# Weight and activation loads of a fused attention and feed-forward kernel put into one gated sequence, with longer and fewer filler matmuls at the start

## The chip, the cores and the metric

The kernel runs on one core of one Trainium2 chip. The metric is device time in microseconds (us) of one execution. A profile is one execution recorded by the hardware profiler; its times count from the first instruction of the span. TensorE is PE (its weight loads are PEld), VectorE is DVE, ScalarE is ACT, GpSimd is POOL, SyncE is SP. SP and POOL issue the DMAs: SP's go through the hardware queue (q1 in the profile), POOL's through the software queue (q0). KB are counted as written to the chip's memory.

## What is computed

Linear attention with a decay per head, in blocks of 64 positions, for 4 batches, 8 heads, 768 positions and a head size of 64, then a feed-forward layer over the 3072 tokens:

```python
for b in range(nb):                                   # blocks of 64 positions
    intra = einsum('bhic,bhjc->bhij', qb, kb) * Dmask
    intra = einsum('bhij,bhjd->bhid', intra, vb)
    inter = einsum('bhid,bhde->bhie', qb * lam_pow, kv_state)
    out[:, :, sl] = intra + inter
    kv_state = lam_block * kv_state + einsum('bhsd,bhse->bhde', kb * rev_pow, vb)
x = out.transpose(0, 2, 1, 3).reshape(3072, 512)
h = x @ w_in                                          # 512 x 2048
g = where(h >= 1, h, where(h <= -1, 0, (h + 1) ** 2 / 4))
y = g @ w_out                                         # 2048 x 512
```

## The kernel before

**Tiling.** Tokens go in 24 chunks `c` of 128; two neighbouring chunks are a pair `m` (0 to 11), which is the unit of loading; four chunks are a stage `s` (0 to 5), the unit of the feed-forward layer. For each pair there are three loads, q, k and v, 512 KB each (`f_load`, L552 for q and L557 for k and v), each into a ring of three buffers. The weights come in eight slices of 512 KB as bf16, converted on the way from float32 by POOL's DMAs: four of w_in (`load_w_in`, L163) by output columns, here called w_in 0 to 3, and four of w_out (`load_w_out`, L167) by rows, w_out 0 to 3.

**Attention of a pair.** q is scaled and cast (`cast_q`, L300), k likewise (`cast`, L292), on DVE or POOL; v is cast on ACT (`cast_v`, L315). In the first three pairs q and k are transposed on PE (`f_tq` L329, `f_t` L322) and copied out by ACT and DVE (`f_qT` L332, `f_kT` L336); later pairs are transposed by DMAs that SP issues (`f_qx` L343, `f_kx` L340). PE then makes the state update `u` (L401; DVE adds it to the state, L407 and L409, ACT copies the state out, L416), the scores in two parts, called A (the first chunk, with half of the state's contribution, L360 and L372) and B (the second chunk); DVE masks the scores (L421); C multiplies by v (L388); ACT copies the result to xT (`f_x`, L428). For a pair in `MERGED` the update u is issued in the same piece as the C of the pair before.

**Feed-forward of a stage.** The first layer (`f_l1`, L439) uses one w_in column tile at a time and writes PSUM tile ph, of which there are two; ACT makes r out of it (L448), DVE makes g in three steps t, w and gT (L458, L464, L469), with three buffers each; the second layer (`f_l2`, L487) accumulates a chunk's 16 row tiles in PSUM tile py, four for each w_out slice; ACT copies it out (L492) and SP stores it. In stage 0 the first layer is done for half a stage (one pair, 256 columns) and one w_in slice at a time, in the order of `L0` (L72). Such a group is 16 matmuls. Below, "group (p, w)" is half p with slice w.

**Order of the work.** Nothing is scheduled by hand in the text: every piece of work is an `Op` (L176) with an engine, a duration, needs and a due time, and `run_plan` (L198) plays them through, always taking the ready one with the earliest due time, and then issues them in that order. Engines run their instructions in that order. `D0` gives the due times of the first four chunks, `l_due` those of the feed-forward pieces, `LEAD`, `APART`, `QXD`, `KXD`, `AD`, `BD` how far ahead of them the attention pieces are due, `LDD` how far ahead the loads. A wrong duration in this plan costs no correctness, only an order that does not suit the chip.

**Loads.** `ORDER` (L69) is the sequence of the first loads: a number is a pair's three loads, a tuple `(0, i)` or `(1, i)` a slice of w_in or w_out. `GATE` (L73) makes one DMA wait until another has landed (`f_load` and `f_w` add that dependency): w_in 0 waits for the q load of pair 1, pair 2's q load for w_in 0, w_out 0 for w_in 2, w_out 2 and pair 3's loads for w_out 0. `W_AFTER` (L196) puts a slice behind a POOL cast.

**Filler matmuls.** In the first 18 us of the plan, `run_plan` fills the idle time of PE in the plan with matmuls of the identity (`warm`, L269 to L274, 256 columns): 80% of the gap at 107 ns each. There are 68 of them, 23 before the first transposes.

Of the kernel before, what the change touches and what calls it, by code (L numbers as in the profile page):

```python
# [23 lines left out]
def kernel(  # L24
# [16 lines left out]
    nc = tc.nc  # L41
# [21 lines left out]
    XT = 6  # L63
    NQT, NQK, RING = 4, 4, 3
    W_IN = (4, 4, 4, 4)
    MERGED = tuple(range(5,12))
    SWITCH = 96
    W_OF = [i for i, n in enumerate(W_IN) for _ in range(n)]
    ORDER = [0, 1, (0, 0), (0, 1), (0, 2), (0, 3), 2, (1, 0), (1, 1), 3, (1, 2), (1, 3)]  # L69
    D0 = (8350, 10000, 15450, 17000)  # L70
    FIRST = [(0, 2), (2, 4)]
    L0 = [(0, 0), (0, 1), (0, 2), (0, 3), (1, 0), (1, 1), (1, 2), (1, 3)]  # L72
    GATE = {(0, 0): ('lq', 1), 2: 0, (1, 0): 2, 3: 4, (1, 2): 4}  # L73
    LORD = {}
    DBG = False

    const = ctx.enter_context(tc.tile_pool(name="const", bufs=1))
# [107 lines left out]

    MMS, FETCH = {"s": 16, "u": 8}, 1300
    FIRST_BYTE = 2750
    LDD, STD = 16000, 3000
    QXD, KXD = 7000, 7000
    AD, BD = (8000, 4000), (4000, 2000)  # L190
    UD, TD = (9000, 9000), (8000, 8000)
    KT_ACT = (1,)
    K_DVE = (0,1,2,3,5)
    ON_DVE = ((0,0),(0,1),(2,1))
    SHARED = (1,(0,1))
    W_AFTER = {1: ("cq", 1, 0)}  # L196

    def run_plan(free):  # L198

        users = {x.key: [] for x in ops}  # L200
        for x in ops:
            x.needs = [OPS[y] for y in x.keys if y in OPS]
            for y in x.needs:
                users[y.key].append(x)
        left = {x.key: len(x.needs) for x in ops}
        topo = [x for x in ops if not x.needs]
        for x in topo:
            for u in users[x.key]:
                left[u.key] -= 1
                if left[u.key] == 0:  # L210
                    topo.append(u)
        assert len(topo) == len(ops)
        for x in reversed(topo):
            d = [u.due - u.ns - x.extra - LAT for u in users[x.key] if not u.dma]
            x.due = min(d + ([x.own] if x.own is not None else []), default=1e9)
            if x.dma or x.key[0] in ("l1", "l2"):
                x.due = x.own
        left = {x.key: len(x.needs) for x in ops}
        ready = {e: [] for e in free}
        for x in topo:  # L220
            if not x.needs:
                ready[x.eng].append((0, x))
        out_seq, xfer, dma_free, fetched = [], [0] * RING, FIRST_BYTE, 0
        while len(out_seq) < len(ops):
            t, e = min((max(free[e], min(r for r, _ in lst), xfer[-RING] if e == "SP" else 0), e)
                       for e, lst in ready.items() if lst)
            r, x = min(((r, x) for r, x in ready[e] if r <= t), key=lambda p: (p[1].due, p[0]))
            ready[e].remove((r, x))
            ns = x.ns + (720 if x.perf and free["POOL"] > t else 0)
            free[e] = t + ns  # L230
            x.t, x.end = t, t + ns + x.extra
            if e == "PE":
                n = fetched + 2 * MMS.get(x.key, MMS.get(x.key[0], 4))
                if n // 256 > fetched // 256:
                    dma_free = max(dma_free, t) + FETCH
                fetched = n
            if x.dma:
                dma_free = max(dma_free, t + (1300 if e == "SP" else 2100)) + x.dma
                x.end = dma_free + (400 if x.key[0] in ("lk", "lv", "lq") and x.key[1] < CPS // 2 else 1000 if x.key[:2] == ("w", 0) else 1400)
                if x.key[0] in ("lk", "lv", "lq") and x.key[1] >= FAR // 2:  # L240
                    x.end += SLACK if x.key[1] >= 5 else NEAR
                if e == "SP":
                    xfer.append(dma_free)
            out_seq.append((t, len(out_seq), x))
            for u in users[x.key]:
                left[u.key] -= 1
                if left[u.key] == 0:
                    ready[u.eng].append((max(y.t if y.eng == u.eng and y.key != u.gate else y.end + (XSL if u.eng == "SP" and y.eng == "POOL" and u.dma in (640, 1280) else LAT) for y in u.needs), u))
        pe_end = WARM[0]
        for t, _, x in sorted(out_seq, key=lambda p: p[:2]):  # L250
            if x.eng == "PE" and pe_end is not None:
                n = int((t - pe_end - 50) * WARM[3] / WARM[2])
                if t > WARM[1]:
                    pe_end = None
                else:
                    pe_end = t + x.ns
                    if DBG and n > 0:
                        print(f"{t / 1e3:9.3f} 0 WARM {n} {x.key}")
                    warm(max(n, 0))
                    if x.key in (("s", 1), ("C", 0)):  # L260
                        hot[0] = None
            if DBG:
                print(f"{t / 1e3:9.3f} {x.due / 1e3:9.3f} {x.eng:5s} {x.ns:6.0f} {x.key}")
            x.fn()

    WARM = (2700, 18000, 107, 0.8)
    hot = [None]

    def warm(n):  # L269

        for _ in range(n):
            if hot[0] is None:
                hot[0] = pp_h.tile([128, MS], F32, name="ph", tag="ph")
            nc.tensor.matmul(hot[0][:, :256], lhsT=ident, rhs=_bc(ident, 1, 2), start=True, stop=True)  # L274

    def mm(*cols):
        return sum(c / 2.4 + 3 for c in cols)
# [232 lines left out]


    T0, STEP = 22000, 1075
    LEAD, APART = 6000, 3000
    PARTS = {1: 2, 2: 2, 4: 1}
    EARLY = 3
    parts = {s: [slice(p * MS // n, (p + 1) * MS // n) for p in range(n)] for s in range(NST) for n in (PARTS.get(s, 1),)}
    parts[0] = [slice(a * C, b * C) for a, b in FIRST]

# [28 lines left out]
    def f_load(c, x, wait):  # L547
        b, s0 = c // NCB, (c % NCB) * C
        if x == 0:
            t = lq.tile([128, H, 2, D], F32, name="x0f", tag="x0f")  # L550
            i = q[b, :, s0:s0 + 2 * C, :].rearrange("h (j e) d -> j h (e d)", e=2)
            d = nc.sync.dma_start(out=t.rearrange("p h e d -> p h (e d)"), in_=i)  # L552
            qkv_ld[c // 2, 0] = t
        else:
            t = ld.tile([128, H, 2, D], F32, name=f"x{x}f", tag=f"x{x}f")
            i = (k, v)[x - 1][b, :, s0:s0 + 2 * C, :].rearrange("h (j e) d -> j h (e d)", e=2)
            d = nc.sync.dma_start(out=t.rearrange("p h e d -> p h (e d)"), in_=i)  # L557
            for e in range(2):
                qkv_ld[c + e, x] = t[:, :, e]
        ld_dma["lq lk lv".split()[x], c // 2] = d.ins.name  # L560
        if wait is not None:
            tc.add_manual_dep(d.ins, w_dma[wait].ins.name, SYNC)

    def f_w(it, wait):
        (load_w_in, load_w_out)[it[0]](it[1])
        if wait is not None:
            tc.add_manual_dep(w_dma[-1].ins, ld_dma[wait] if isinstance(wait, tuple) else w_dma[wait].ins.name, SYNC)


    order = list(ORDER)  # L570
    order += [m for m in range(NCH // 2) if m not in order]

    w_seen, last_c, pos_ = [], None, 0
    for it in order:
        if isinstance(it, tuple):
            gated = GATE.get(it)
            need = [("w",) + w_seen[-1] if w_seen else None, W_AFTER.get(len(w_seen))]
            key = None
            if gated is not None:
                key = gated if isinstance(gated, tuple) else ("w",) + w_seen[gated]  # L580
                need.append(key)
            add(("w",) + it, "POOL", 900, lambda it=it, wait=gated: f_w(it, wait), need, due=pos_ * 1e-3,
                dma=2560)
            if key is not None:
                OPS[("w",) + it].gate = key
            w_seen.append(it)
            pos_ += 1
            continue
        m, gated = it, GATE.get(it)
        od = o_due(2 * m + 1)  # L590
        for x in LORD.get(m, (0, 1, 2)):
            need = [("w",) + w_seen[gated] if gated is not None else ("w",) + w_seen[-2] if len(w_seen) > 1 else None]
            need += [[("cq", m - LQ, 0), ("cq", m - LQ, 1), ("cq", m - LQ, 9)], [("cast", 2 * (m - LD) + 1, 1), ("cast", 2 * (m - LD) + 1, 9)],
                     [("cast", 2 * (m - LD) + 1, 2)]][x]
            add(("lq lk lv".split()[x], m), "SP", 700, lambda m=m, x=x, wait=gated: f_load(2 * m, x, wait), need,
                due=pos_ * 1e-3 if m < EARLY else od - LDD, dma=1850)
            pos_ += 1

    NPB = NCH // 2
    for m in range(NPB):  # L600
# [155 lines left out]
```

## Time and profile before

| | |
|---|---|
| median of 13 runs | 220.34 us (218.81 to 221.85) |
| the profiled execution's own time | 219.83 us |
| its span | 218.1 us, so 1.7 us lie around it |
| PE busy | 206.9 us (95%) |
| DVE, ACT, POOL busy | 150.3, 115.2, 59.9 us |
| first matmul of the first layer | 19.57 us |
| DMA, share of 16 engines by q1 and q0 | 62.3% and 11.8% |
| x0f (q) loads, waited for by POOL's casts | 33.5 us in 8 waits |
| granted TensorE clock | 1.0 |

A busy PE is not PE at its peak, and fillers count as busy. DMA issue times stand on the issuing engine; the time from issue to landing of a single DMA is read by asking for its tile in a window that holds only that issue.

### The profile page before, as it was taken

How to read it: one execution, taken by the hardware profiler on the slowest of the kernel's cores; microseconds unless marked ns; L12 is line 12 of the kernel's file. 1: busy time of each engine (PE TensorE's matmuls, PEld its weight loads, DVE VectorE, ACT ScalarE, POOL GpSimd, SP SyncE). 2: the span in 40 equal slices, each digit the busy share in tenths (PEclk: the TensorE clock that was granted, in tenths of full speed). 3: DMA queues.
4: the chain of work that ended last, by engine and by line, in shares of the span. 5: the costliest groups of instructions: out<-in, count | busy, mean ns of one | idle time of the engine just before them, and what ended most of it. 6: DMA issues, size and time to landing. Idle time of an engine off the chain costs nothing.

```text
span 218.1 us, 5513 instructions
## 1 busy us (share of the span) xinstructions
PE 206.9 (95%) x2343; PEld 120.9 (55%) x2343; DVE 150.3 (69%) x235; ACT 115.2 (53%) x200; POOL 59.9 (27%) x63
## 2 busy tenths in 40 slices
PE   3998978999999999999999999999999999999994
PEld 2767757557546767756654454544544444444442
DVE  4584965989980899899899969668467354554301
ACT  3257657527616767295657556564634643555020
POOL 5390233449082652265363421000000000000000
DMA  6999999999899999999999957311011101110122
GB/s 163 290 237 197 253 238 223 218 296 96 225 254 236 208 255 182 256 227 281 166 286 221 268 156 200 44 53 48 0 51 48 38 13 48 48 48 12 39 96 96
DMA packets 64587, 34.43 MB, mean 158 GB/s; under 512 B 20403, under 2 KB 61619, under 8 KB 64563
## 3 DMA queue, kind: packets, MB, share of 16 engines
q1 hardware_dynamic: 60336, 29.89, 62.3%
q0 software_dynamic: 4224, 4.19, 11.8%
q8 instruction: 18, 0.29, 0.6%
q14 instruction: 7, 0.05, 0.1%
q10 hardware_dynamic: 2, 0.00, 0.0%
HBM read 27.26 MB, written 6.29 MB: 154 GB/s over the span
## 4 chain that ended last, share of the span: by engine, by line
PE 83%; DMA 9%; ACT 2%; POOL 2%; SPq 1%; DVE 1%; issue 1%; ACTq 0%
PE ph L439 36%; PE py L487 36%; DMA w_in_sb<-in_moe_w_in_dram 6%; DMA x0f<-in_q_dram 3%; PE px L388 3%; PE ps L360 2%; PE px L372 2%; PE py L481 1%; POOL w_in_sb L163 1%; PE ps L401 1%; ACT r L448 1%; SPq L557 1%; ACT xT L428 1%; DVE sc L421 1%; POOL qs L300 0%
## 5 line engine op out<-in xcount | busy, mean ns | idle before, releaser
L439 PE MATMUL ph<-xT,w_in_sb 128*128 128x256 bf16 (+1 forms) x576 | 95.9, 308 | 2.7 <-ACT xT L428 1.1
L448 ACT ACTIVATE r<-ph,one 128x512 bf16<-128x512 f32 x96 | 65.6, 688 | 51.8 <-PE ph L439 44.9
L487 PE MATMUL py<-w_out_sb,gT 128*128 128x512 bf16 x368 | 90.6, 380 | 0.0
L439 PEld LDWEIGHTS <-w_in_sb 128*128 128x128 bf16 x576 | 54.8, 98 | 32.9 <-issue 2.1
L487 PEld LDWEIGHTS <-gT 128*128 128x128 bf16 x368 | 34.4, 98 | 38.0
L458 DVE TENSOR_SCALAR t<-r 128x1024 bf16<-128x1024 bf16 x48 | 28.0, 584 | 21.8 <-ACT r L448 21.8
L464 DVE TENSOR_TENSOR w<-r,t 128x1024 bf16<-128x1024 bf16 x48 | 40.1, 835 | 1.3
L469 DVE TENSOR_TENSOR gT<-w,t 128x1024 bf16<-128x1024 bf16 x48 | 38.4, 801 | 1.3
L300 POOL TENSOR_TENSOR qs<-x0f,tab_q 128x512 bf16<-128x512 f32 (+1 forms) x22 | 26.1, 1200 | 45.7 <-DMA x0f<-in_q_dram 33.5
L292 POOL TENSOR_TENSOR ks<-x1f,tab_p 128x512 bf16<-128x512 f32 (+1 forms) x20 | 25.1, 1272 | 14.5 <-DMA x1f<-in_k_dram 9.2
L421 DVE TENSOR_TENSOR sc<-ps,causal 128x512 bf16<-128x512 f32 x23 | 15.8, 688 | 10.9 <-PE pt L360 9.5
L492 ACT COPY osb<-py 128x512 f32<-128x512 f32 x23 | 13.5, 586 | 16.5 <-PE py L487 15.5
L428 ACT CAST xT<-px 128x512 bf16<-128x512 f32 x24 | 13.0, 587 | 13.1 <-PE px L388 9.1
L421 DVE TENSOR_TENSOR sc<-pt,causal 128x512 bf16<-128x512 f32 x22 | 14.9, 679 | 0.0
L315 ACT CAST v<-x2f 128x512 bf16<-128x512 f32 x24 | 13.8, 620 | 1.1 <-DMA x2f<-in_v_dram 1.1
L274 PE MATMUL ph<-ident 128*128 128x256 bf16 x68 | 10.9, 318 | 0.0
L360 PE MATMUL ps<-qT,kT 64*64 64x128 bf16 x184 | 10.6, 220 | 0.0
L360 PEld LDWEIGHTS <-kT 64*64 64x64 bf16 x384 | 7.7, 107 | 4.3 <-issue 4.0
L416 ACT CAST ub<-state 128x256 bf16<-128x256 f32 x19 | 7.7, 405 | 4.4 <-DVE state L409 2.4
L360 PE MATMUL pt<-qT,kT 64*64 64x128 bf16 x176 | 9.7, 219 | 0.0
L409 DVE TENSOR_TENSOR state<-state,ps 128x256 f32<-128x256 f32 x8 | 3.3, 417 | 7.9 <-PE pt L401 6.9
L274 PEld LDWEIGHTS <-ident 128*128 128x128 bf16 x68 | 7.3, 114 | 2.1 <-issue 0.4
(59 smaller groups left out, 88.4 us busy)
## 6 DMA issues: line engine op xcount, KB each, us to landing
x0f<-in_q_dram SPq DMA_DIRECT2D x12, 512.0 KB, 5.6
x1f<-in_k_dram SPq DMA_DIRECT2D x12, 512.0 KB, 6.6
x2f<-in_v_dram SPq DMA_DIRECT2D x12, 512.0 KB, 7.2
out_dram<-osb SPq DMA_DIRECT2D x23, 256.0 KB, 2.1
w_in_sb<-in_moe_w_in_dram POOLq DMA_DIRECT2D x4, 512.0 KB, 8.9
w_out_sb<-in_moe_w_out_dram POOLq DMA_DIRECT2D x4, 512.0 KB, 10.2
kT<-ks SPq DMA_TRANSPOSE x18, 4.3
out_dram<-osb SPq DMA_DIRECT2D x1, 192.0 KB, 1.9
```

Of the source, the lines that this page charges most:

```text
L274: nc.tensor.matmul(hot[0][:, :256], lhsT=ident, rhs=_bc(ident, 1, 2), start=True, stop=True)
L292: eng.tensor_tensor(ho(ks[c])[:, bs], hs(qkv_ld[c, 1])[:, bs], ho(_bc(tab, 2, D))[:, bs], op=AX.mult)
L300: eng.tensor_tensor(ho(qs[m, e])[:, bs], hs(qkv_ld[m, 0][:, :, e])[:, bs], ho(_bc(tab_q[:, e, m % (NCB // 2), :], 2, D))[:, bs], op=AX.mult)
L360: nc.tensor.matmul(pst[a, r][HD[i], b, :], lhsT=kT[a][HD[r], b, HD[i]], rhs=q_cols(2 * m + i, b, HD[r]), start=True, stop=True)
L421: nc.vector.tensor_tensor(sc_sb[c][:, g], pst[c, g], _bc(causal2[:, c % 2], 1, HP), op=AX.mult)
L428: nc.scalar.copy(out=o, in_=px[:, c % 2].rearrange("p h (e j) -> p h j e", e=2))
L439: nc.tensor.matmul(ph[:, j * m:(j + 1) * m], lhsT=w_in_sb[:, ko, (ni + j) * 128:(ni + j + 1) * 128], rhs=xT[s][:, ko, tok], start=(ko == 0 ...
L448: nc.scalar.activation(out=o, in_=x, func=AF.Relu, bias=one[:, 0:1])
L458: nc.vector.tensor_scalar(t, r, 0.5, 1.0, op0=AX.mult, op1=AX.min)
L464: nc.vector.tensor_tensor(w, r, t, op=AX.subtract)
L469: nc.vector.tensor_tensor(gT[s][:, f - RW * n:f, tok].rearrange("p (a b) m -> p a b m", a=RW), w.rearrange("p a (b m) -> p a b m", m=m), t ...
L487: nc.tensor.matmul(py_t[s, ms], lhsT=gT[s][:, ko, ms * 128:(ms + 1) * 128], rhs=w_out_sb[:, ko, :], start=(ko == 0), stop=(ko == FO - 1))
```

## The change

The first loads become one list, `xfers`, of single DMAs on both queues. Wherever the list passes from one queue to the other, the first DMA on the new queue waits for the landing of an earlier one of the list: three places back for POOL's DMAs, two for SP's (`BACK`). The list is: the loads of pairs 0 and 1; w_in 0, 1, 2; the loads of pair 2; w_in 3 and w_out 0 to 3; the loads of pair 3. So w_in 0 waits for the q load of pair 1 (as before), pair 2's q load for w_in 1, w_in 3 for pair 2's q load, and pair 3's q load for w_out 2. w_in 0 and 1 stand behind POOL's two q casts of pair 1. Stage 0's first layer takes slices 0 to 2 of both halves before slice 3. The first q cast and the second k cast are no longer split between DVE and POOL. Fillers have 256 columns before 8.3 us of the plan and 512 after it, 213 ns each; 22 are left (9 of 256 columns and 13 of 512), 5 of them before the first transposes. Due times, `MERGED` (now with pair 4) and the engines of some casts change with it.

```diff
-    MERGED = tuple(range(5,12))
+    MERGED = tuple(range(4,12))
-    ORDER = [0, 1, (0, 0), (0, 1), (0, 2), (0, 3), 2, (1, 0), (1, 1), 3, (1, 2), (1, 3)]
-    D0 = (8350, 10000, 15450, 17000)
+    ORDER = [0, 1, (0, 0), (0, 1), (0, 2), 2, (0, 3), (1, 0), (1, 1), (1, 2), (1, 3), 3]
+    D0 = (8350, 8000, 15450, 15000)
-    L0 = [(0, 0), (0, 1), (0, 2), (0, 3), (1, 0), (1, 1), (1, 2), (1, 3)]
-    GATE = {(0, 0): ('lq', 1), 2: 0, (1, 0): 2, 3: 4, (1, 2): 4}
+    L0 = [(0, 0), (0, 1), (0, 2), (1, 0), (1, 1), (1, 2), (0, 3), (1, 3)]
+    GATE = {}
+    BACK = {True: 3, False: 2}
...
-    LDD, STD = 16000, 3000
-    QXD, KXD = 7000, 7000
-    AD, BD = (8000, 4000), (4000, 2000)
+    LDD, STD = 25000, 3000
+    QXD, KXD = 10000, 10000
+    AD, BD = (7000, 5500), (3000, 2500)
-    KT_ACT = (1,)
-    K_DVE = (0,1,2,3,5)
+    KT_ACT = (1,3)
+    K_DVE = (0,1,2,3,4,5)
-    SHARED = (1,(0,1))
-    W_AFTER = {1: ("cq", 1, 0)}
+    SHARED = ()
+    W_AFTER = {0:("cq",1,0), 1: ("cq", 1, 1)}
...
+                w = 256 if t < WARM[4] else 512
...
-    WARM = (2700, 18000, 107, 0.8)
+    WARM = (4200, 18000, 213, 0.8, 8300)
-            nc.tensor.matmul(hot[0][:, :256], lhsT=ident, rhs=_bc(ident, 1, 2), start=True, stop=True)
+            nc.tensor.matmul(hot[0][:, :w], lhsT=ident, rhs=_bc(ident, 1, w // 128), start=True, stop=True)
...
-    LEAD, APART = 6000, 3000
+    LEAD, APART = 3000, 3000
...
+    xfers = []
+    for it in ORDER:
+        if isinstance(it, int):
+            xfers += [(n, it) for n in ("lq", "lk", "lv")]
+        else:
+            xfers.append(it if it[0] in ("lq", "lk", "lv") else ("w",) + it)
+    early = len(xfers)
+    xfers += [(n, m) for m in range(NCH // 2) for n in ("lq", "lk", "lv") if (n, m) not in xfers]
+    w_at, last_w, last_hw = {}, None, {}
+    for n, x in enumerate(xfers):
+        sw = x[0] == "w"
+        gate = None
+        if n and sw != (xfers[n - 1][0] == "w"):
+            back = BACK[sw]
+            gate = GATE.get(x, xfers[n - back] if n >= back else None)
+        if sw:
+            need = [last_w, W_AFTER.get(len(w_at)), gate]
+            add(x, "POOL", 900, lambda x=x, gate=gate: f_w(x[1:], gate), need, due=n * 1e-3, dma=2600)
...
+            need = [gate] if n < early else [last_w]
...
+            add(x, "SP", 700, lambda m=m, i=i, gate=gate: f_load(2 * m, i, gate), need,
+                due=n * 1e-3 if n < early else o_due(2 * m + 1) - LDD, dma=1850)
```

More of the change, by code (lines that the diff above doesn't have):

```diff
@@ L65 @@
     W_IN = (4, 4, 4, 4)
-    MERGED = tuple(range(5,12))
+    MERGED = tuple(range(4,12))
     SWITCH = 96
     W_OF = [i for i, n in enumerate(W_IN) for _ in range(n)]
-    ORDER = [0, 1, (0, 0), (0, 1), (0, 2), (0, 3), 2, (1, 0), (1, 1), 3, (1, 2), (1, 3)]
-    D0 = (8350, 10000, 15450, 17000)
+    ORDER = [0, 1, (0, 0), (0, 1), (0, 2), 2, (0, 3), (1, 0), (1, 1), (1, 2), (1, 3), 3]
+    D0 = (8350, 8000, 15450, 15000)
     FIRST = [(0, 2), (2, 4)]
-    L0 = [(0, 0), (0, 1), (0, 2), (0, 3), (1, 0), (1, 1), (1, 2), (1, 3)]
-    GATE = {(0, 0): ('lq', 1), 2: 0, (1, 0): 2, 3: 4, (1, 2): 4}
-    LORD = {}
+    L0 = [(0, 0), (0, 1), (0, 2), (1, 0), (1, 1), (1, 2), (0, 3), (1, 3)]
+    GATE = {}
+    BACK = {True: 3, False: 2}
     DBG = False
@@ L258, in run_plan @@
                         print(f"{t / 1e3:9.3f} 0 WARM {n} {x.key}")
-                    warm(max(n, 0))
+                    warm(max(n, 0), w)
                     if x.key in (("s", 1), ("C", 0)):
@@ L264, in run_plan, with warm @@
             x.fn()
-    WARM = (2700, 18000, 107, 0.8)
+    WARM = (4200, 18000, 213, 0.8, 8300)
     hot = [None]
-    def warm(n):
+    def warm(n, w):
         for _ in range(n):
@@ L512 @@
     T0, STEP = 22000, 1075
-    LEAD, APART = 6000, 3000
+    LEAD, APART = 3000, 3000
     PARTS = {1: 2, 2: 2, 4: 1}
-    EARLY = 3
     parts = {s: [slice(p * MS // n, (p + 1) * MS // n) for p in range(n)] for s in range(NST) for n in (PARTS.get(s, 1),)}
@@ L561, in f_load, with dma_name @@
         if wait is not None:
-            tc.add_manual_dep(d.ins, w_dma[wait].ins.name, SYNC)
+            tc.add_manual_dep(d.ins, dma_name(wait), SYNC)
+    def dma_name(key):
+        return w_dma[w_at[key[1:]]].ins.name if key[0] == "w" else ld_dma[key]
     def f_w(it, wait):
@@ L566, in f_w @@
         if wait is not None:
[L567 to L592, printed above, removed]
-            need += [[("cq", m - LQ, 0), ("cq", m - LQ, 1), ("cq", m - LQ, 9)], [("cast", 2 * (m - LD) + 1, 1), ("cast", 2 * (m - LD) + 1, 9)],
[L594 to L597, printed above, removed]
@@ new lines, in f_w @@
+            tc.add_manual_dep(w_dma[-1].ins, dma_name(wait), SYNC)
+    xfers = []
[16 more added lines that the diff above has]
+            add(x, "POOL", 900, lambda x=x, gate=gate: f_w(x[1:], gate), need, due=n * 1e-3, dma=2600)
+            OPS[x].gate = gate
+            w_at[x[1:]] = len(w_at)
+            last_w = x
+        else:
+            m, i = x[1], ("lq", "lk", "lv").index(x[0])
+            need = [gate] if n < early else [last_w]
+            need += [[("cq", m - LQ, 0), ("cq", m - LQ, 1), ("cq", m - LQ, 9)], [("cast", 2 * (m - LD) + 1, 1), ("cast", 2 * (m - LD) + 1, 9)],
+                     [("cast", 2 * (m - LD) + 1, 2)]][i]
+            if n and n < early and xfers[n - 1][0] != "w":
+                need.append(xfers[n - 1])
+            add(x, "SP", 700, lambda m=m, i=i, gate=gate: f_load(2 * m, i, gate), need,
+                due=n * 1e-3 if n < early else o_due(2 * m + 1) - LDD, dma=1850)
+            OPS[x].gate = gate
```

## The prediction

> **What bounds the kernel now.** First the slices and the chain of the page:
>
> ```profile
> PE   3998978999999999999999999999999999999994
> DMA  6999999999899999999999957311011101110122
> ...
> PE 83%; DMA 9%; ACT 2%; POOL 2%; SPq 1%; DVE 1%; issue 1%; ACTq 0%
> ```
>
> From slice 10 (about 49 us) on PE is full, so the end is the time at which PE becomes full plus the work then left. The 9% of DMA lie ahead of that. So the question is how early PE has done a given amount of useful work near 48 us. The chain cut to 8 to 50 us shows what it waits for (start, duration, what):
>
> ```profile
> 14.20 13.51 DMA w_in_sb<-in_moe_w_in_dram
> 27.71 0.05 issue
> 27.75 1.06 PE ph L439 x8
> ...
> 46.23 1.83 PE py L487 x8
> 48.06 1.97 PE ph L439 x17
> ```
>
> At 48.06 PE has done stage 0's first layer (8 groups of 16 matmuls), A, B and C of pair 2 and 24 matmuls of the second layer. I call this **the mark**. The timeline from 14 to 32 us shows two holes before it:
>
> ```profile
> 24.02 1.56 POOL L167 DMA_DIRECT2D w_out_sb<-in_moe_w_out_dram  x2 [7.99 <-DMA w_in_sb<-in_moe_w_in_dram]
> ...
> 27.75 1.16 PE L439 MATMUL ph<-xT,w_in_sb 128*128 128x256 bf16 x9 [1.02 <-DMA w_in_sb<-in_moe_w_in_dram]
> ...
> 28.84 1.07 ACT L428 CAST xT<-px 128x512 bf16<-128x512 f32 x2 [1.95 <-PE ph L439]
> ...
> 29.96 2.30 PE L439 MATMUL ph<-xT,w_in_sb 128*128 128x256 bf16 x19 [1.05 <-ACT xT L428]
> ```
>
> PE waits for w_in 3, and then for pair 1's xT, which stands on ACT behind an r that itself needs w_in 3. Further holes of PE before the mark: about 0.7 at 18, 0.4 at 34 and 1.2 at 37 to 38.8, where ACT's v cast of pair 2 waits for its load (at 37.02) and holds up ACT's r.
>
> The last view is of single DMAs, each w_in slice asked for alone: issue start, then issue to landing:
>
> ```profile
> L163 POOL DMA_DIRECT2D w_in_sb<-in_moe_w_in_dram x1: 932/932/932, 10.7 to 10.7; - x1
> DMA to landing us min/median/max: 6.0/6.0/6.0
> ...
> L163 POOL DMA_DIRECT2D w_in_sb<-in_moe_w_in_dram x1: 760/760/760, 14.2 to 14.2; - x1
> DMA to landing us min/median/max: 13.5/13.5/13.5
> ```
>
> So w_in 0 lands at 16.7 and w_in 3 at 27.7. By the same view w_in 1 and 2 land at 20.3 and 23.75, w_out 0 to 3 at 32.85, 36.4, 41.9 and 45.6. Consecutive slices land 3.5 to 3.7 apart: **3.58 a slice** (20.3-16.7; 36.4-32.85 is 3.55). Pair 2's q and k land at 28.2 and 31.8, v by 37.0; pair 3's at 39.2, 45.9 and 47.6. With no weights in flight, loads land 1.8 apart (45.9, 47.6, 49.4, 51.1).
>
> **The start.** Fillers before the first transposes:
>
> ```profile
> 4.16 4.84 PE L274 MATMUL ph<-ident 128*128 128x256 bf16 x23
> ...
> 5.09 1.44 DVE L300 TENSOR_TENSOR qs<-x0f,tab_q 128x512 bf16<-128x512 f32 x2 [0.55 <-DMA x0f<-in_q_dram]
> ```
>
> The q casts are done at 6.54, but 23 fillers hold PE until 8.8. Five fillers end at 4.16+5x0.21=5.2, so the transposes start with the casts. Unsharing the casts costs DVE nothing: 692 ns for a whole one alone against 835 beside POOL, so both end at 5.09+2x0.69=6.47. Scores of chunk 0 come at about 8.85 instead of 11.06. What hides most of it: v of pair 0 still lands at 8.64, pair 1's k at 12.23 and v at 13.99 (nothing here changes before 10 us), and ACT is then in line: qT to 14.5, two v casts 1.15, ub 0.4, xT 0.58, kT 0.58, ub 0.4, xT 0.58: xT of pair 0 is ready at 18.1 instead of 18.44. POOL's second q cast of pair 1 moves ahead of w_in 1 (13.6 instead of 16.0), which lets A of pair 1 go before the first group: group (0,0) starts at 18.7 with A done, against 19.57 without. **Gain here about 1.3, at PE.**
>
> The clock: 23 fillers in 4.84 us are 210 ns each, eight at 9.28 us take 1.03, 129 each, so PE speeds up near 8.5, though the PEclk column says 1.00 throughout. With gaps between its first matmuls that may come later. Bounds: nothing, or one more such stretch of 4.3 us in which some 2 us of real work (16 transposes, two scores and an update) take twice as long. I take nothing: A of pair 1 waits for casts that end at 13.6 and for ACT, which cover it; the upper end is 0.5. The Trainium skill ("TensorE: Matmul & The Clock Gate", Parts 1 and 4) speaks against thinner fillers: the clock is released by some 3.4 us of sustained work and transposes do not count. By it the slow stretch could last to the first groups and cost an estimated 1.7 us more.
>
> **The weights.** POOL casts (1.06) before w_in 0, so it issues at about 11.6 instead of 10.73; pair 1's v, landing at 13.99, hides part of this. Between 16.7 and 17.6 I take 17.3. Then w_in 1 at 20.9, w_in 2 at 24.4 (3.58 a slice; before 20.3 and 23.75). Pair 2's q, issued when w_in 1 lands, 4.2 later than before: before, it was issued at 16.7 behind three slices and landed 0.5 after the last; now only w_in 2 is ahead of it, so 24.9. That opens the gate of w_in 3. The gate costs what w_in 0 shows: 6.0 from issue to landing against 3.58 in a stream, 2.4 for the hand-over. w_in 3 lands at 24.9+6.0=30.9, 3.2 later than now. Behind it on POOL stand the four w_out issues (4x0.78) and the q cast of pair 2, at about 29; its user on PE comes at 31.3. Then w_out at 34.5, 38.1, 41.6, **45.2**. Pair 2's v has at most w_in 3 beside it, 28.4 to 33, instead of 37.
>
> The skill ("DMA: Bandwidth & Descriptors", "Issuing engines are not separate DMA queues") says that both queues share the same 16 engines, so separating them makes no bandwidth. The trace agrees: mixed they move 217 GB/s from 37.2 to 43 us, weights alone 195 from 17 to 20; by that rule only order and the hand-overs count.
>
> **PE to the mark,** 1.75 a group (the chain's x16), 0.86 per four L487, 0.35 to 0.5 a piece of attention: (0,0) 18.7 to 20.45; B; (0,1) 20.9 (w_in 1) to 22.65; C to 23.1; (0,2) waits for w_in 2, 24.4 to 26.15, a new wait of 1.3; half 1's slices 0 to 2 to 31.4, its xT long ready: both old holes are gone. Then q's transposes; k's wait for ACT's v casts and qT copies (2.3 behind pair 2's v): slice 3 at 33.6 if v lands by 31. With the rest, the fourth quarter of w_out is wanted at 43.8, and it lands at 45.2. A late v pushes this only if it lands after 32. That place is the mark: **45.2 to 45.5 against 48.06, a gain of 2.6.** It is capped by w_out 3, which before was never waited for.
>
> **Given back later.** Pair 3's q waits for w_out 2 (41.6) instead of w_out 0 (32.85). It lands about 45.8, then at 1.8 each k 47.6, v 49.4 and pair 4's three by 54.8, which now stand on SP ahead of pair 3's transposing DMAs; these landed at 53.7 (2.5 behind the load before) and 55.1, so now 57.3, 58.8, 60.3. A of pair 3 was at 61.7 and comes at 59.1 to 60: cover shrinks from 6.6 to almost nothing. Likewise pair 4: about 68.5 wanted at 69 to 70, before 66.9 for 72.7. Bounds: 0 to 2; I take 0.4. Later pairs had 7 to 14 us of cover. `MERGED` and the cast engines move work on engines with idle time; bounds from the small holes of PE after 50 us (3 us in all): ±0.5, taken as 0.
>
> **Sum:** 219.83-2.6+0.4 = **217.6**, against the profiled execution; the median of the runs shown is 0.5 above it, so 218.1 on that footing. Its own range, with the cast of v, the clock and the later holes: 216.3 to 218.7.
>
> **Rivals.**
> (1) *Weights faster.* If the slices after w_in 3 come at the mean rate of the queue (512 KB at 195 GB/s, 2.7 us), w_out 3 lands at 41.7 and PE's own 43.8 decides: 219.83-4.3 = 215.5. Against it: all six steps within w_in and within w_out are 3.46 or more.
> (2) *Cover gone.* The gain to the mark comes, but pairs 3 and 4 each wait 1 us or v lands at 33: 219.2, no change to speak of. For it: cover of 0.3 to 1.
> (3) *Slower: the gate of w_in 3 opens late.* If pair 2's q trails as it did (28.2), the gate opens 3.3 later: w_in 3 at 34.2, w_out 3 at 48.5, and with pair 2's k and v still mixed in (0.8 each: 8.75 us for two slices and two loads from 28.2 to 36.95) 50.1, so the mark is 2.1 late: 221.9. It decides from a q landing at 27.5 on. For it: a load issued at 16.7 took 11.5. Against it: only one slice is then ahead.
>
> **How the numbers follow.** Forecast 0.45, (1) 0.10, (2) 0.20, (3) 0.25. A measurement tells about 0.5% (1.1 us) from no change: faster 0.55, same 0.20, slower 0.25. Range: from about (1) to about (3), with half of each taken as lying outside (0.05 and 0.12): 215.6 to 221.9.
>
> **What would show it.** w_in 3 landing near 31, pair 2's q near 25; the first L439 at 18.7 and no wait for w_in 3 or for xT near 29; a wait of PE for w_in 2 near 23 and for w_out 3 near 45; kT of pair 3 landing just before its A. Wrong if q of pair 2 lands after 27.5, if w_out 3 lands later than 47, if fillers still run at 213 ns after 10 us, or if PE waits over 1 us for a transposing DMA at 60 to 70.

## The result and the profile after

| | before | after |
|---|---|---|
| median, us (executions) | 220.86 (48) | 218.03 (11) |
| lowest to highest, us | 218.81 to 224.78 | 216.92 to 219.16 |
| profiled execution / its span, us | 219.83 / 218.1 | 218.51 / 216.8 |

The ratio is **0.988, 95% interval 0.9854 to 0.9907**: faster by 1.2%. Ratios leave out executions more than 1.5% above the fastest of their kernel; medians are of all. Between the two profiled executions only 1.3 us lie; the other half of the median's gain is dealt with under "late settings" below. In the functions, line numbers of the kernel after are one higher than before (L487 is L488).

The page of the kernel after, its row of PE, its row of DMA and its chain:

```profile
PE   3896797999999999999999999999999999999993
...
DMA  6999999999997999799999996511101101110022
...
PE 84%; DMA 7%; DVE 3%; POOL 2%; ACT 2%; issue 0%; DVEq 0%
```

Both rows of PE, this one and that of the kernel before, stand at 9 from the eighth digit on (38 us), so the row does not show when PE becomes full. Its busy time from 38 to 50 us does: 12.0 of 12 us here, 11.3 before. The chain's share of DMA falls from 9 to 7%. The kernel's chain from 8 to 50 us (start, duration, what):

```profile
14.35 10.94 DMA w_in_sb<-in_moe_w_in_dram
...
25.34 1.06 PE ph L440 x8
...
26.42 1.08 ACT xT L429 x2
...
30.57 2.12 DVE ks L293 x2
...
38.86 0.86 PE py L488 x4
...
42.03 0.86 PE py L488 x4
...
43.35 2.69 PE py L488 x12
46.05 0.57 PE px L389 x32
46.62 1.83 PE py L488 x8
```

The DMA piece now ends with w_in **2** at 25.29; w_in 3 and w_out are not in the chain. The mark, 24 L488 done, is at 46.62+0.9=**47.5**, where the prediction had 45.2 to 45.5 and before 48.06. What PE waited for from 14 to 60 us (total, times, longest):

```profile
PE px L373 <- ACT xT L429: 1.7, 1, 1.7
PE ph L440 <- ACT xT L429: 1.1, 1, 1.1
PE pt L330 <- DVE t L459: 0.7, 1, 0.7
PE pt L323 <- ACT qT L333: 0.7, 1, 0.7
PE ph L440 <- DMA w_in_sb<-in_moe_w_in_dram: 0.6, 1, 0.6
```

The wait for w_in 3 is gone, that for the second half's xT stands, and four are new: A of pair 1 ahead of the first group, w_in 2, and two at pair 2's transposes. Useful work on PE (its matmuls in the two traces, fillers left out) is level with before at 41 us, 0.2 ahead at 46, 0.6 at the mark, 1.0 at 72 and 1.3 to 1.4 from 94 us on.

The weights. Asked for alone, w_in 3 (first pair of lines) and the four of w_out:

```profile
L163 POOL DMA_DIRECT2D w_in_sb<-in_moe_w_in_dram x1: 742/742/742, 27.4 to 27.4; - x1
...
DMA to landing us min/median/max: 5.5/5.5/5.5
...
L167 POOL DMA_DIRECT2D w_out_sb<-in_moe_w_out_dram x4: 747/765/777, 28.1 to 30.3; - x4
...
DMA to landing us min/median/max: 8.6/11.2/13.9
```

w_in 3 lands at 32.8, w_out 0 at 28.09+8.6=36.7 and w_out 3 at 30.3+13.9=44.2: 2.5 a slice, not 3.58. The last quarter of w_out is wanted at 47.5.

### The profile page after: what moved, and what is told of

Same layout as the page of the kernel before. It is cut to its first block, busy times and chain, and to the rows that moved or that the text cites. A ratio compares the mean times of both kernels' runs of the same rounds, so it can differ in the third digit from the quotient of the medians.

```text
span 216.8 us, 5405 instructions
## 1 busy us (share of the span) xinstructions
PE 203.6 (94%) x2297; PEld 116.9 (54%) x2297; DVE 144.6 (67%) x235; ACT 116.9 (54%) x201; POOL 55.4 (26%) x60
## 4 chain that ended last, share of the span: by engine, by line
PE 84%; DMA 7%; DVE 3%; POOL 2%; ACT 2%; issue 0%; DVEq 0%
PE py L488 38%; PE ph L440 35%; DMA w_in_sb<-in_moe_w_in_dram 5%; PE px L389 3%; PE ps L361 2%; DMA x0f<-in_q_dram 2%; PE px L373 2%; PE py L482 1%; PE ps L402 1%; DVE ks L293 1%; POOL qs L301 1%; DVE t L459 1%; PE pt L323 1%; POOL w_in_sb L163 1%; DVE qs L301 1%; PE py L330 1%
## 5 line engine op out<-in xcount | busy, mean ns | idle before, releaser
L488 PE MATMUL py<-w_out_sb,gT 128*128 128x512 bf16 x368 | 90.4, 380 | 0.0
L440 PEld LDWEIGHTS <-w_in_sb 128*128 128x128 bf16 x576 | 54.9, 98 | 31.9 <-issue 1.2
L488 PEld LDWEIGHTS <-gT 128*128 128x128 bf16 x368 | 34.5, 98 | 37.8
L459 DVE TENSOR_SCALAR t<-r 128x1024 bf16<-128x1024 bf16 x48 | 24.6, 512 | 25.0 <-ACT r L449 25.0
L465 DVE TENSOR_TENSOR w<-r,t 128x1024 bf16<-128x1024 bf16 x48 | 37.8, 787 | 1.4
L470 DVE TENSOR_TENSOR gT<-w,t 128x1024 bf16<-128x1024 bf16 x48 | 37.3, 776 | 1.3
L301 POOL TENSOR_TENSOR qs<-x0f,tab_q 128x512 bf16<-128x512 f32 x21 | 24.7, 1193 | 42.9 <-DMA x0f<-in_q_dram 27.2
L293 POOL TENSOR_TENSOR ks<-x1f,tab_p 128x512 bf16<-128x512 f32 x18 | 22.2, 1251 | 23.9 <-PE pt L402 18.6
L422 DVE TENSOR_TENSOR sc<-ps,causal 128x512 bf16<-128x512 f32 x23 | 15.9, 691 | 16.2 <-PE pt L361 13.9
L373 PE MATMUL px<-qT,ub 64*64 64x128 bf16 x152 | 6.5, 222 | 1.7 <-ACT xT L429 1.7
L389 PEld LDWEIGHTS <-v 64*64 64x64 bf16 x384 | 5.8, 107 | 4.1 <-issue 4.0
L389 PE MATMUL px<-sc,v 64*64 64x128 bf16 x384 | 7.7, 219 | 0.0
```

The source lines that it names most:

```text
L293: eng.tensor_tensor(ho(ks[c])[:, bs], hs(qkv_ld[c, 1])[:, bs], ho(_bc(tab, 2, D))[:, bs], op=AX.mult)
L301: eng.tensor_tensor(ho(qs[m, e])[:, bs], hs(qkv_ld[m, 0][:, :, e])[:, bs], ho(_bc(tab_q[:, e, m % (NCB // 2), :], 2, D))[:, bs], op=AX.mult)
L389: nc.tensor.matmul(px[HD[g], i, j, :], lhsT=v_sb[(2 * m + e) % NV][HD[i], 2 * j + g, :], rhs=sc_sb[2 * m + e][HD[i], r, b, :], start=(c % ...
L422: nc.vector.tensor_tensor(sc_sb[c][:, g], pst[c, g], _bc(causal2[:, c % 2], 1, HP), op=AX.mult)
L440: nc.tensor.matmul(ph[:, j * m:(j + 1) * m], lhsT=w_in_sb[:, ko, (ni + j) * 128:(ni + j + 1) * 128], rhs=xT[s][:, ko, tok], start=(ko == 0 ...
L459: nc.vector.tensor_scalar(t, r, 0.5, 1.0, op0=AX.mult, op1=AX.min)
```

## The experiments

**Theory after the result:** up to about 36 us two chains end at PE's first layer, the *start* (transposes, casts, xT) and the *loads* (w_in, pair 2). The new dummies (the filler matmuls) shorten the first and the new sequence with the new order shortens the second, so each alone gains little; the late settings add some. **Rivals:** the start alone makes the gain; the loads alone do; all of it comes behind 50 us. All times below were taken beside the kernel before. Its own median lay between 220.70 and 221.32 in the three sets of executions, so ratios are compared here, and not medians across rows.

| kernel | median us | ratio to before, interval |
|---|---|---|
| before + new dummies | 220.4 | 0.9998 (0.9963 to 1.0033) |
| after, old dummies | 219.69 | 0.9989 (0.9953 to 1.0024) |
| after, narrow dummies | 217.55 | 0.9885 (0.9844 to 0.9927) |
| after, two xT tiles | 216.95 | 0.9865 (0.9824 to 0.9905) |
| after, both of these | 217.27 | 0.9846 (0.9803 to 0.9889) |
| before + dummies + order | 223.96 | 1.0141 (1.0089 to 1.0193) |
| after, old order | 223.87 | 1.0153 (1.0099 to 1.0208) |
| after, pair 3 early | 217.88 | 0.9876 (0.983 to 0.9922) |
| after, late settings old | 219.14 | 0.9931 (0.99 to 0.9961) |
| after, MERGED old | 219.21 | 0.9921 (0.9884 to 0.9957) |
| before + late settings | 222.5 | 0.9995 (0.9943 to 1.0047) |

### The new dummies alone, and the change without them

Before, with the diff's new `WARM` and `warm` only:

```diff
-    WARM = (2700, 18000, 107, 0.8)
+    WARM = (4200, 18000, 213, 0.8, 8300)
```

> The kernel before with the new dummy matmuls alone; loads, slices and order stay the old ones. In the kernel after, the first transposes came at 5.89 us instead of 8.84, but its five dummies of 512 columns at 10.43 took 427 ns each, and u of chunk 0 came at 12.39. Theory A (the start's gain is eaten by the dummies at a clock that is still slow, and the weights decide afterwards): transposes again at 5.9, the first group no earlier than 19.3, and the time within 0.3% of before (ratio 0.997 to 1.003). Theory B (the earlier start itself makes the gain): the first group 0.9 us or more earlier than before, ratio 0.993 or less.

Measured 0.9998. The timeline of PE in this kernel:

```profile
18.49 1.04 PE L439 MATMUL ph<-xT,w_in_sb 128*128 128x256 bf16 x8
...
27.71 1.16 PE L439 MATMUL ph<-xT,w_in_sb 128*128 128x256 bf16 x9 [1.66 <-DMA w_in_sb<-in_moe_w_in_dram]
```

Theory A foresaw the time and not the way: the first group comes 1.08 us **earlier** than before (19.57), so the dummies do not eat the start's gain; the wait for w_in 3 eats it (1.66 against 1.02), and from 27.7 on the two profiles run within 0.1 us of each other to 60 us.

After, with the old dummies:

```diff
-    WARM = (4200, 18000, 213, 0.8, 8300)
+    WARM = (2700, 18000, 107, 0.8, 99999)
```

> The kernel after with the old dummy matmuls: 256 columns each, counted at 107 ns. Loads, slices and order stay the new ones. Theory A (weights decide): the transposes go back to 8.8, but the clock is fast by 8.5 to 9, so that the first group stays within 0.6 us of the kernel after (19.9), and the time within 0.3% of it: ratio to before 0.985 to 0.991. Theory B (the start makes the gain): the first group comes 0.8 us or more later than in the kernel after, and the ratio rises to 0.992 or more.

Measured 0.9989: theory A fell here. With the loads in the new sequence the start does bound. A of pair 1, which opens PE's work on the first layer, in the timeline of PE:

```profile
21.18 0.31 PE L373 MATMUL px<-qT,ub 64*64 64x128 bf16 x8 [1.59 <-ACT xT L429]
```

In the kernel after:

```profile
19.47 0.31 PE L373 MATMUL px<-qT,ub 64*64 64x128 bf16 x8 [1.75 <-ACT xT L429]
```

It is 1.7 us later with the old dummies, and 1.5 of these are still there at the end of the profile. In the kernel before the same A came at 20.54, so old dummies in the new plan give a start 0.6 us later still than the old one, and not exactly the old one. So the two parts of the change only pay **together**: with the old loads a faster start waits for w_in 3, with the old start the new loads wait for xT.

### The clock at the start, and the xT hole

After, with all dummies 256 columns wide:

```diff
-    WARM = (4200, 18000, 213, 0.8, 8300)
+    WARM = (4200, 18000, 213, 0.8, 99999)
```

> The kernel after with all dummy matmuls 256 columns wide, in the same number. The five at 10.43 took 2.03 us at 512 columns. Theory A: the dummies stand in the path of the start, u of chunk 0 comes 0.9 us earlier (11.5), the first group at 19.0 to 19.4, and PE then waits for w_in 2 (landing at 25.3) by as much more: the time changes by 0 to 0.5 us, ratio 0.985 to 0.988. Rival: with less work the clock becomes fast later than 13 us, the first group comes at 20 or later, and the time rises by 0.3 us or more (ratio 0.990 or above).

A of pair 1 comes at 18.52 instead of 19.47, as theory A has it, though the first half of the rival came true too: PE was slow for longer, not shorter. PE in this kernel, then the same four transposes in the kernel after:

```profile
10.36 1.25 PE L275 MATMUL ph<-ident 128*128 128x256 bf16 x5
...
12.71 0.59 PE L330 MATMUL py<-ident,qs 128*128 128x128 bf16 x4
```

```profile
13.37 0.38 PE L330 MATMUL py<-ident,qs 128*128 128x128 bf16 x4 [0.31 <-DVE state L408]
```

The narrow dummies took 250 ns each and the transposes 0.59 us, so PE was slow here until about 13.1; in the kernel after it was fast from about 12. What the narrow dummies saved is work ahead of u of chunk 0 while PE is slow: five of them took 1.25 us, the five wide ones 2.03. The time (0.9885) cannot be told from that of the kernel after; the profiled execution is 1.7 us ahead, 0.95 from the start and 0.66 because its w_in 2 landed at 22.6 rather than 25.3, which the dummies do not touch. In the nine profiles of the kernel after and its variants w_in 2 landed anywhere from 22.6 to 25.3, the kernel after itself being the latest; a difference of 0.7 us between two single profiles can be chance.

After, with stage 0's xT in two tiles (and the same choice where layer 1 reads it):

```diff
+    xT0 = [const.tile([128, KO, 2 * C], BF16, name=f"xTh{i}") for i in range(2)]
...
-        if sx not in xT:
+        if sx and sx not in xT:
...
-        o = xT[sx][:, :, off:off + C].rearrange("p h (j e) -> p h j e", e=2)
+        o = (xT[sx][:, :, off:off + C] if sx else xT0[off // (2 * C)][:, :, off % (2 * C):off % (2 * C) + C]).rearrange("p h (j e) -> p h j e", e=2)
```

> The kernel after with stage 0's transposed x in two tiles, one for each half, in place of one tile with both halves. In the kernel after, ACT waited 1.53 us before the second half's xT copy (at 26.42) for a layer 1 matmul of the first half, which reads other columns of the same tile, and PE then waited 1.05 us at 27.55. Theory: that wait is by tile and not by data, so with two tiles the copy comes before 26.0 and PE's wait at 27.5 falls below 0.3 us; PE then meets the weights sooner, so 0.3 to 1.1 us of the time go, ratio 0.983 to 0.987. Rival 1: the hole goes, but PE is then held by slice 3 or w_out and the time stays (0.987 to 0.990). Rival 2: the wait is by data or by ACT's order and PE's hole stays at 1 us.

ACT's copy in the kernel after, then ACT's and PE's timelines with two tiles:

```profile
26.42 1.07 ACT L429 CAST xT<-px 128x512 bf16<-128x512 f32 x2 [1.53 <-PE ph L440]
```

```profile
24.28 1.07 ACT L430 CAST xTh<-px 128x512 bf16<-128x512 f32 x2
```

```profile
24.28 4.93 PE L441 MATMUL ph<-xTh,w_in_sb 128*128 128x256 bf16 x42
```

The copy no longer waits and PE runs through 42 matmuls. The wait was by tile: the copy writes columns that no earlier matmul reads. This profile is 2.3 us ahead of that of the kernel after by 29 us: 0.5 from a clock that came up sooner, 0.7 from w_in 2 (23.2), 1.1 from the hole. The ratio, 0.9865, fits the theory, but its interval also holds rival 1.

Both together:

> The kernel after with stage 0's transposed x in two tiles and all dummy matmuls 256 columns wide, both in one. Alone, the tiles gave a ratio of 0.9865 (profile 2.2 us ahead of that of the kernel after), the narrow dummies 0.9885 (first group 0.95 us earlier). If both shorten the same chain, that of the start up to the second half's xT, they add: 1.0 to 2.2 us less than the kernel after, ratio 0.978 to 0.984. If the weights or pair 2's casts bound PE behind them (two waits of 0.84 us for qT copies and casts stand at 31 to 35 in every variant), only one of the two is seen: 0.984 to 0.988.

0.9846 lies in the second case's range, near its edge to the first, and its interval reaches into both. It is the lowest ratio here, against 0.988; the intervals overlap, so that it beats the kernel after is likely and not shown. Its profile has the next bound: PE waits 0.9 us for w_in 2 (24.5) and still twice 0.7 at pair 2's transposes. These profiles also show where the time between them and the kernel after lay at the start. The five dummies ahead of u of chunk 0, in the kernel after and in this one:

```profile
10.43 2.03 PE L275 MATMUL ph<-ident 128*128 128x512 bf16 x5
```

```profile
10.39 0.75 PE L276 MATMUL ph<-ident 128*128 128x256 bf16 x5
```

Half the columns take a third of the time: PE was still slow in the first (some 400 ns for 512 columns) and fast from about 10.7 in the second. With the same narrow dummies it was slow until about 13.1 in the profile with these alone: when PE becomes fast differs from one execution to another by more than these dummies move it.

### Sequence and order

Before, with the new dummies and the new order of stage 0's first layer:

```diff
-    L0 = [(0, 0), (0, 1), (0, 2), (0, 3), (1, 0), (1, 1), (1, 2), (1, 3)]
+    L0 = [(0, 0), (0, 1), (0, 2), (1, 0), (1, 1), (1, 2), (0, 3), (1, 3)]
```

> The kernel before with the new dummy matmuls and the new order of stage 0's first layer (fourth slice after the second half's third); loads and their gates stay old. With the dummies alone the first group was 1.1 us earlier, and PE gave it back in a wait of 1.86 us for w_in 3 at 25.8 to 27.7. Theory C (the gated sequence is needed: an earlier start is only kept if pair 2's loads come before w_in 3): the wait for w_in 3 goes, but pair 2's q lands at 28 as before and its k and v at 31 to 34, so PE waits 1.5 us or more for its transposes or its cast v between 30 and 38; ratio to before 0.996 to 1.008. Rival (dummies and order make the whole gain, and the loads' sequence does nothing): no wait of over 0.9 us between 30 and 38, ratio 0.985 to 0.992.

Measured 1.0141, slower than theory C's 1.008. PE and ACT in their timelines:

```profile
39.19 1.03 PE L439 MATMUL ph<-xT,w_in_sb 128*128 128x256 bf16 x8 [3.02 <-ACT r L448]
```

```profile
37.41 1.14 ACT L315 CAST v<-x2f 128x512 bf16<-128x512 f32 x2 [2.46 <-DMA x2f<-in_v_dram]
38.46 1.26 ACT L448 ACTIVATE r<-ph,one 128x512 bf16<-128x512 f32 x2
```

Pair 2's v lands after 37; its cast holds ACT, the r behind it frees layer 1's sums late, and PE waits 3.0 us: what theory C named. About 2 us more go between 50 and 55 us, in holes of 0.6 for masked scores and 1.2 for an xT copy.

After, with the old order (the same lines the other way round):

> The kernel after with the old order of stage 0's first layer (fourth slice of the first half ahead of the second half), so that w_in 3, which the gated sequence puts behind pair 2's loads and which lands at 31.6 to 32.8, is wanted at about 27. With the new order on the old loads the time rose to a ratio of 1.014 (PE waited 3.2 us for pair 2 at 36). Theory C (sequence and order only work together): PE waits 3.5 to 5.5 us for w_in 3, the two waits of 0.84 us at 33 to 35 and the wait for the second half's xT go in return, and the time rises by 1 to 3.5 us over the kernel after: ratio 0.993 to 1.004. Rival (the order is free to choose, PE only swaps one wait for another): within 0.3% of the kernel after.

Measured 1.0153, well over the 1.004 expected. PE waits 4.8 us, about as much as expected, yet not for w_in 3 (landed at 31.9) but for the casts of pair 2's q, whose transposes now stand ahead of the other groups; and nothing is given back. The timelines of PE and POOL, then a table of the whole core by stretches (the number after the five engines is the granted clock):

```profile
31.19 0.61 PE L330 MATMUL pt<-ident,qs 128*128 128x128 bf16 x4 [3.67 <-POOL qs L301]
32.95 0.61 PE L330 MATMUL pt<-ident,qs 128*128 128x128 bf16 x4 [1.15 <-DVE qs L301]
```

```profile
27.08 2.98 POOL L167 DMA_DIRECT2D w_out_sb<-in_moe_w_out_dram  x4
30.04 1.09 POOL L301 TENSOR_TENSOR qs<-x0f,tab_q 128x512 bf16<-128x512 f32 x1
```

```profile
28.00:28.50 0.50, 0.00 (x0) 0.00 (x0) 0.23 (x1) 0.24 (x1) 0.50 (x1) 1.00 0.67 66
28.50:30.00 1.50, 0.00 (x0) 0.00 (x0) 1.50 (x2) 0.33 (x1) 1.50 (x3) 0.51 1.13 183
30.00:38.00 8.00, 5.66 (x34) 4.32 (x35) 4.25 (x7) 2.81 (x6) 1.13 (x2) 0.50 1.20 189
...
38.50:40.00 1.50, 1.50 (x26) 1.13 (x25) 1.38 (x4) 0.74 (x2) 0.00 (x0) 0.91 1.25 203
```

q itself had landed at 26.05; its cast on POOL stands behind the issues of w_in 3 and the four w_out slices. So the wait comes from the order of POOL's work under this plan, which theory C did not name. From 28.5 to about 38.8 the clock is at 0.50; 16 layer 1 matmuls take 3.31 us in it, at 35.91, and 1.92 after it, at 39.52. This adds to the loss, as in the last experiment, where the clock is at 0.50 from 40.6 to 44.0. By the ratios sequence and order are one change: either without the other is worse than neither (1.0141, 1.0153).

After, with pair 3's q gated by w_out 0 again:

```diff
-    GATE = {}
+    GATE = {('lq', 3): ('w', 1, 0)}
```

> The kernel after with pair 3's q gated by w_out 0, as before, in place of w_out 2: its three loads run beside w_out 1 to 3. Alone on their queue these three slices landed 2.43 to 2.57 us apart; in the kernel before, beside loads, 3.5 to 3.7. Theory E (what stretched the slices is the other queue's loads): w_out 1 to 3 land 3.3 or more apart while pair 3's loads run, w_out 3 at 46 to 48 instead of 44.2, and PE, which wants its last quarter at about 45.8, waits up to 1.6 us for it: ratio 0.988 to 0.995. Rival (the slices' pace was set by their own issues or queue): steps stay at 2.4 to 2.7, w_out 3 by 45, pair 3 five us earlier, and the time stays or falls: 0.985 to 0.989.

The last two w_out slices, asked for alone:

```profile
L167 POOL DMA_DIRECT2D w_out_sb<-in_moe_w_out_dram x2: 770/774/777, 29.4 to 30.2; - x2
...
DMA to landing us min/median/max: 12.8/14.3/15.8
```

They land at 42.3 and 46.0, so the steps are 2.45, 3.0 and 3.7 us, with 0, 98 and 792 KB of pair 3's loads moved during them. The last step fits theory E's pace; one of 3.0 does not need it, since in the kernel with both of the last two changes a step of 2.90 passed with no load beside it. The time does not follow: 0.9876, and PE does not wait for w_out, wanted at 47.7. No gain from the separation of *these* loads is seen. That pair 2 going ahead of w_in 3 is what counts is likely; it was not tested by itself.

### The late settings

Where the gain behind 50 us comes from. After, with three late settings old:

```diff
-    MERGED = tuple(range(4,12))
+    MERGED = tuple(range(5,12))
...
-    LDD, STD = 25000, 3000
-    QXD, KXD = 10000, 10000
+    LDD, STD = 16000, 3000
+    QXD, KXD = 7000, 7000
```

> The kernel after with three of its late settings old: pair 4's state update stands alone again (MERGED from 5), the loads are due 16 us ahead instead of 25, and the transposing DMAs 7 us instead of 10. Everything up to about 45 us stays. In the kernel with the dummies alone, 1.8 us were lost at 60 to 66: VectorE's multiplications of stage 1 took 1.41 us instead of 0.69 while POOL cast pair 4's q, and PE waited for the masked scores. Theory D (the rest of the gain over the profiled pair, some 1.4 us at the median, comes from pair 4's casts no longer falling on that stretch of VectorE): with the late settings old, up to 1.5 us come back: ratio 0.990 to 0.995. Rival (the gain is made ahead of 45 us, and the late settings only keep it): within 0.3% of the kernel after, 0.985 to 0.991.

0.9931: theory D's size, but not its place. This profile runs 0.8 us ahead of that of the kernel after up to 69 us, PE does not wait for masked scores at 60 to 66, and it ends 0.1 behind: some 0.9 us go behind 69 us. With `MERGED` alone put back:

> The kernel after with one late setting old: pair 4's state update stands alone (MERGED from 5); the due times of loads and transposing DMAs stay new. With all three late settings old the ratio was 0.9931. Theory D1 (the merge itself carries that part): 0.991 to 0.995. Theory D2 (the earlier due times carry it): 0.985 to 0.990.

0.9921: D1's size, the merge seems to carry it; the interval just reaches D2's. Its profile is 0.4 ahead of that of the kernel after at 60 us and 0.9 behind from 111 on. Of the mechanism there is one place to show. In that kernel PE waits at 105, for VectorE, which multiplies while POOL casts (from 101.48 to 104.15); timelines of PE and VectorE:

```profile
105.08 0.21 PE L361 MATMUL pt<-qT,kT 64*64 64x128 bf16 x1 [0.82 <-DVE state L410]
```

```profile
102.05 1.20 DVE L465 TENSOR_TENSOR w<-r,t 128x1024 bf16<-128x1024 bf16 x1
103.28 1.42 DVE L470 TENSOR_TENSOR gT<-w,t 128x1024 bf16<-128x1024 bf16 x1
104.62 0.41 DVE L410 TENSOR_TENSOR state<-state,pt 128x256 f32<-128x256 f32 x1
```

The same settings alone on the kernel before:

> The kernel before with the three late settings of the kernel after alone (MERGED from 4, loads due 25 us ahead, transposing DMAs 10); dummies, early loads, slices and order stay old. Theory D (the late settings are worth some 1 us by themselves): ratio 0.992 to 0.997. Rival (they only fit a plan in which the early part is shorter): 0.998 to 1.006.

0.9995: the rival's size. The interval (0.9943 to 1.0047) also reaches theory D's 0.997, so that here too the parts only work together is likely and not shown.

The kernel before once more, for a second profile:

> The kernel before once more, unchanged, for a second profile. Its median over many executions is 220.9 us against 219.8 of the one profiled. If theory D holds, an execution near or over the median shows pair 4's q landing before about 60 us, POOL's casts of it on VectorE's multiplications at 59 to 64, and a wait of PE of 1 us or more for masked scores at 60 to 66; if the profile is again near 219.8, q lands after 60 and the wait is absent. Rival: an execution that is slower loses its time ahead of 45 us, in waits for w_in or for pair 2.

218.89 us, still faster than the median. Pair 4's q lands at 59.8 and no wait for masked scores follows, which is the second branch of theory D but for the landing (after 60 was expected). The run was not near the median, so it does not test what theory D says of such a one. That *was* seen in the kernel with the new dummies alone, which equals before in all else; its profiled execution took 221.69. POOL, VectorE and PE there:

```profile
58.82 2.49 POOL L300 TENSOR_TENSOR qs<-x0f,tab_q 128x512 bf16<-128x512 f32 x2 [4.29 <-issue]
61.27 2.67 POOL L292 TENSOR_TENSOR ks<-x1f,tab_p 128x512 bf16<-128x512 f32 x2
```

```profile
60.33 1.26 DVE L458 TENSOR_SCALAR t<-r 128x1024 bf16<-128x1024 bf16 x1
61.62 1.41 DVE L464 TENSOR_TENSOR w<-r,t 128x1024 bf16<-128x1024 bf16 x1
63.07 1.41 DVE L469 TENSOR_TENSOR gT<-w,t 128x1024 bf16<-128x1024 bf16 x1
```

```profile
65.14 0.21 PE L360 MATMUL ps<-qT,kT 64*64 64x128 bf16 x1 [1.15 <-DVE sc L421]
```

q landed 1.9 us earlier than in the profile of before, POOL's casts fell on four of VectorE's operations, and 1.8 us were lost between 60 and 66. That before's typical execution loses its further 1 us in this way is likely, and stays open.

## Why the prediction came out, step by step

The forecast and its sign hold: on the footing of the median 218.1 against 218.03. On that of the profiled execution it was 217.6 against 218.51. The sum behind it does not hold: a gain of 2.6 at the mark and a loss of 0.4 behind it were a gain of 0.6 and a further gain of 0.7 between the profiles. The rest comes from which executions were profiled: that of before lay 1.0 us below the median of 220.86, that of after 0.5 above its own. So the mechanism (two holes ahead of the first layer's later groups, cured by an earlier start and a new sequence of loads) is right in part, and that the figure came out so closely is partly luck.

The prediction took PE as full from slice 10 (49 us); its own row shows it from the eighth digit, 38 us. The sum does not use that number.

- **The start.** The transposes came at 5.89 (5.8 predicted). The first group came at 19.93, not 18.7. The term that was mis-sized is the slow clock, taken as nothing with an upper end of 0.5: the five wide dummies ahead of u took 2.03 us in place of the 1.07 that the plan gives them (213 ns each), and narrow ones moved A of pair 1 by 0.95 us. The skill's rule gave an estimated 1.7 us more; the 0.95 lies between the two.
- **Fillers still slow after 10 us** was named as a sign against the forecast and did occur (some 400 ns for 512 columns until about 12; three of them took 0.82 us in all at 14.52). Its price was about 1 us, and less in the time.
- **Weights.** w_in 0 landed at 18.9, where 16.7 to 17.6 was expected. "3.58 a slice" failed: 2.5 for w_out alone. Rival (1)'s pace, 2.7, was right, but its time was not, since PE wanted the last quarter at 47.5 and not 43.8. That w_out 3 caps the gain is wrong: it landed 3.3 us before it was wanted.
- **Pair 2 and w_in 3.** q landed at 27.1, against 24.9, close to the 27.5 from which rival (3) was to decide; w_in 3 at 32.8, against 30.9. It cost nothing, because w_in 3 is now wanted after pair 2's transposes (about 36). Rival (3) priced a late q through w_out 3 (48.5 to 50.1 at 3.58 a slice); w_out 3 landed at 44.2.
- **Both old holes gone.** One is. That xT stood on ACT behind an r that needs w_in 3 was wrong: the wait stayed when no r ahead of it needed w_in 3 any more, and two tiles removed it in the kernel after.
- **"Slice 3 at 33.6"** came at 36.5: w_in 2 0.9 later (25.3 against 24.4), the xT hole 1.05, and two waits of 0.67 at pair 2's transposes, which the prediction had not seen; together 3.3, the rest of my row being 0.4 too long.
- **Given back later.** Pair 3's transposing DMAs landed at 58.6 to 59.5 as predicted (57.3 to 60.3), and no wait followed. `MERGED`, "taken as 0" within 0.5, was worth about 0.4% (0.9921 against 0.988), some 0.9 us, with intervals that overlap.

## What to carry to other kernels

Where two chains meet, a change to one shows nothing until the other is moved too: test the parts of a change alone *and* left out, since here each alone gave no change or a loss. Before a hole is counted as cured, find the instruction that releases it; a wait can be on a neighbour in the same tile. And a load that lands late is only as bad as the time at which it is wanted in the *new* order.

## What the runs showed of the hardware

- At the start the granted clock reads 1.00 in the kernel after, though five wide dummies took 2.03 us at 10.43 and three took 0.82 at 14.52: the reading does not show that PE is slow there. Later it does. With the old order a hole of 3.7 us in PE (27.5 to 31.2) halved the granted clock from 28.5, and it came back at 38.8, though PE was busy again from 33. In the experiment before it, after a hole of 3.0 us, it was halved for 3.4 us, when PE was already at work again; after holes of up to 1.75 us it stayed at 1.00. The Trainium skill ("TensorE: Matmul & The Clock Gate", Part 1) puts both ways at about 3.4 us, seen through windows that run freely; the size of the holes agrees roughly, and so does the second slow stretch; the first was three times as long (10.2 us).
- VectorE's 128x1024 bf16 multiplication, which reads two operands from SBUF, took 0.68 to 0.69 us in all 75 cases of the kernel after without a POOL cast beside it. The 16 that began while a cast ran took 0.70 to 1.42, and each ended 0.55 us after the end of that cast; the lines above show it twice (63.07+1.41=64.48 against 61.27+2.67=63.94, and 104.70 against 104.15). In the five cases in which the multiplication began first it took its 0.69, and POOL's cast took 1.48 to 1.57 us instead of 1.04. Masking from PSUM took 0.68 either way. The skill ("SBUF — State Buffer", "SBUF: two separate sides") says that the two engines share one pair of ports, that whichever starts first has it for its whole instruction and that the other is blocked; these rows agree.
- In the kernel after w_out 1 and 2 (512 KB each) landed 2.43 and 2.54 us behind the slice before with no load beside them, and w_out 3 came 2.57 behind with 180 KB of loads. With pair 3 early w_out 3 came 3.72 behind, with 792 KB of loads in that time. Loads are not the only thing that stretches a step: from w_in 0 to w_in 1 it took 2.3 to 3.8 us in the 14 profiles, and in none of them did another queue move a packet in that time.
